# Attention and a gated feed-forward on one core: the values' products ahead of both score steps

## The chip, the cores and the metric

The kernel runs on one core of a Trainium2 chip. The core has five engines that run side by side and meet through semaphores: TensorE (PE in the profile; its weight loads are PEld), VectorE (DVE), ScalarE (ACT), GpSimd (POOL) and SyncE (SP), which issues the transfers here. The metric is the device time of one execution in microseconds (us); less is better.

## The reference

Two stages, in fp32. First attention over 8 batches of 8 heads, with 576 positions and 64 numbers a head. The mask is causal in blocks of 64: a row of block i sees all columns of blocks 0 to i.

```python
scores = scale * np.matmul(q, k.transpose(0, 1, 3, 2))
mask = block_i >= block_j
scores = np.where(mask, scores, -1000000000.0)
scores = scores - np.max(scores, axis=-1, keepdims=True)
attn = np.exp(scores)
attn = attn / (np.sum(attn, axis=-1, keepdims=True) + 1e-09)
return np.matmul(attn, v)
```

The heads of a batch are joined to x (576 x 512), and a gated feed-forward with a residual runs over each batch:

```python
h = gelu(x @ w_in)                     # 512 -> 1024, tanh form
u, v = h[..., :512], h[..., 512:]
v_n = (v - mean(v)) / sqrt(var(v) + 1e-06) * g_ln
v_s = einsum('ts,bsd->btd', w_sg, v_n) + b_sg[None, :, None]
return x + (u * v_s) @ w_out           # 512 -> 512
```

## The kernel before, in words

*Slots.* Attention runs two heads at a time: 32 pairs of heads, one pair a slot, four slots to a batch. Slots 0 to 3 are `opening_slot` (L728), slots 4 to 31 are `slot` (L766). In slot n the kernel finishes the attention of pair n, computes the scores and the softmax of pair n+1, and fills TensorE's time between with pieces of the feed-forward of batches whose attention is done. The tiles of the feed-forward are called accv (first product, v half), accu (u half), accs (the product along the sequence) and acco (the last product).

*A pair's scores.* The 576 rows are cut into five row tiles, 0 to 4 (64 rows, then four times 128); tile i needs 64 + 128 i columns. `Scores.products` (L329) computes them in parts. The contraction is over the 64 numbers of a head, so the two heads lie in the two row halves of the TensorE array: head 0 in rows 0 to 63, head 1 in rows 64 to 127, each writing a bank of its own. Each number is split into a high and a low fp32r part, and three matmuls (high by high, low by high, high by low) add up. `first` (L399) does two parts: 256 columns of tile 4 with tile 1, then the other 320 columns of tile 4 with tile 0. `second` (L403) does tile 3 and then tile 2. A part takes two banks, one for each head, and 6 matmuls for each tile in it: 24 in `first`, 12 in `second`. After the products of a part, `softmax` (L387) issues the maximum on VectorE (`maximum`, L351: adds the mask, writes the scores to SBUF as `prob` and their negated maximum as `negm`) and the exponential on ScalarE (`exponent`, L372, with the sum of each row).

*A pair's values.* In the slot that follows, TensorE turns the probabilities: `va.turn` (L426) makes pA0, pA1, pB0, pB1 and pC, which ScalarE or VectorE copies to SBUF as ptA, ptB and ptC. `turn_sums` (L448) turns the diagonal blocks and the reciprocals of the sums into the banks pd and pe; ScalarE copies both into one tile, rb. `Values.products` (L467) then multiplies the turned probabilities with v: 60 matmuls, head 0 into the left half of the array's columns and head 1 into the right half, row tiles 4 down to 0, into the bank ob; row tile 0 goes to a free part of pe. `normalise` (L484) multiplies ob and that part of pe with the turned reciprocals on VectorE, which gives x, and issues its store (`spill`) on SP's queue. `split` makes the high and low parts of x (xh, xl) later.

*Order of work.* From slot 4 on, TensorE alone is held to the order of the program (`written`, L829, used by `pin`, L83). The order on VectorE, ScalarE and GpSimd is made by a planner which simulates the program with costs of its own; work that comes earlier in the program goes first where both are ready. All PSUM tiles come from one pool of eight banks (L80). `hole(k)` issues the next k pieces of feed-forward; a slot does so after the first transposes, after the second, after `turn_sums` (one piece) and at its end, with counts from `PLAN` and `FIRST` (L718). `load_share` (L709) issues shares of the preparation of weights in slots 4 to 8, at four places of a slot; the third of them, which stands right behind the second score step, has a count of zero in every slot of `WS`.

Of the kernel before, what the change touches and what calls it, by code (L numbers as in the profile page):

```python
# [20 lines left out]
def kernel(  # L21
# [82 lines left out]
    def load_qk(n):  # L104
        b, h = PAIRS[n]
        q_f = sp.tile([P, S], F32, tag="q_f", name="q_f", bufs=1)
        k_f = sp.tile([P, S], F32, tag="k_f", name="k_f", bufs=1)
        nc.sync.dma_start(q_f, qT[b, h : h + 2].rearrange("a d s -> (a d) s"))
        nc.sync.dma_start(k_f, kT[b, h : h + 2].rearrange("a d s -> (a d) s"))
        raw[n] = (q_f, k_f)  # L110

    def split_qk(n):
        out = []
        for x, t in zip(raw.pop(n), "qk"):
            hi = sp.tile([P, S], F32R, tag=t + "h", name=t + "h", bufs=1)
            lo = sp.tile([P, S], F32R, tag=t + "l", name=t + "l", bufs=1)
            if n == 0:
                copy("v" if t == "q" else "a", hi, x)
                vector.tensor_tensor(lo, x, hi.bitcast(F32), op=ALU.subtract)
            else:  # L120
                copy("g", hi, x)
                behind["G"] = gpsimd.tensor_tensor(lo, x, hi.bitcast(F32), op=ALU.subtract)
            out += [hi, lo]
        qk[n] = out

    def load_v(n):
        b, h = PAIRS[n]
        v_f, v_d = vals[n] = v_bufs[n % 2]
        lo, hi = slice(0, BLK), slice(BLK, P)
        for a, r in ((0, lo), (1, hi)):  # L130
            cols = slice((h + a) * D, (h + a + 1) * D)
            x = v[b, : (NT - 1) * P, cols].rearrange("(j p) d -> p j d", p=P)
            if a == 0:
                nc.sync.dma_start(v_f[:, :, r], x)
            else:
                nc.sync.dma_start(v_f[lo, :, r], x[hi])
                nc.sync.dma_start(v_f[hi, :, r], x[lo])
            nc.sync.dma_start(v_d[r, : NT - 1, r], x[lo])
            nc.sync.dma_start(v_d[r, NT - 1, r], v[b, S - TAIL :, cols])
# [162 lines left out]
    def weight_step():  # L302

        while weight_half() is False:
            pass
# [200 lines left out]
    def run_side(k):  # L506

        while k > 0 and side and side[0][0] != "G":
            k -= 1
            side.popleft()[1]()  # L510

    def run_gelu():

        if side and side[0][0] == "G":
            side.popleft()[1]()
# [176 lines left out]
    def hole(k=1):  # L692

        while k > 0 and work:
            try:
                next(work[0])
                k -= 1
            except StopIteration:
                work.popleft()
# [9 lines left out]
    def load_share(n, k):  # L709

        if n in WS:
            with ExitStack() as order:
                for ins in behind.values():
                    order.enter_context(tc.issue_after(ins.ins))
                for _ in range(WS[n][k]):
                    weight_step()
# [5 lines left out]
    def split_pending():  # L722

        for f in pending:
            f()
        pending.clear()
# [39 lines left out]
    def slot(n, va):  # L766
        nx = n + 1 < N
        k = 6 if n // Q == 1 else 3
        g = [int(x) for x in (FIRST if n // Q == 1 else PLAN)[n % Q]]
        if n + 1 < N:  # L770
            load_v(n + 1)
        if n + 2 < N:
            load_qk(n + 2)
        va.turn("A0")
        va.turn("A1")
        hole(g[0])
        run_side(k)
        split_pending()
        load_share(n, 0)
        va.turn("B0")  # L780
        va.turn("B1")
        hole(g[1])
        run_side(k)
        va.turn("C")
        va.turn_sums()
        hole(g[2])
        run_gelu()
        load_share(n, 1)
        if nx:
            nx = Scores(n + 1)  # L790
            nx.first()
        va.products()
        va.normalise()
        if nx:
            nx.second()
        load_share(n, 2)
        if n == Q + 1:
            run_side(2 * NT + 1)
        if n % Q == Q - 1:
            va.split()  # L800
        else:
            pending.append(va.split)
        nv = None
        if nx:
            nv = Values(n + 1, nx)
            nv.inverse()
        if n + 2 < N:
            split_qk(n + 2)
        load_share(n, 3)
        for _ in range(g[3]):  # L810
            hole()
            run_side(k)
        return nx, nv
# [12 lines left out]
    va = Values(0, sc)  # L826
    for n in range(N):
        if n == Q:
            written.intersection_update("P")  # L829
        sc, va = (opening_slot if n < Q else slot)(n, va)  # L830
        if n % (H // 2) == H // 2 - 1:
            v_, u_, s_, o_ = feed_forward(PAIRS[n][0])
            work.extend([v_, u_, *last_o, s_])
            last_o[:] = [o_]
# [47 lines left out]
```

## Time and profile before

| | |
|---|---|
| median of 3 runs | 758.8 us (758.28 to 758.92) |
| the profiled execution | 758.84 us, of which the span from the first to the last instruction is 757.0 us |
| TensorE busy | 735.8 us |
| VectorE busy | 474.8 us |
| ScalarE busy | 425.3 us |
| GpSimd busy | 305.0 us |
| granted TensorE clock, mean | 0.993 |

A row of the profile names the engine, the line, the operation and the tiles as out<-in. Nearly every instruction goes through one helper and so bears the line L60; groups are told apart by their tiles. For a matmul the shape of the array in use stands after the tiles: 128\*128 is the whole array, 64\*128 a row half, 128\*64 a column half. Matmuls are pipelined: the length in a row is longer than the distance to the next start. An idle time stands in brackets behind a row, with what ended it.

### The profile page before, as it was taken

What the parts mean: (1) busy time and instruction counts of PE and PEld (TensorE: products, weight loads), DVE (VectorE), ACT (ScalarE), POOL (GpSimd) and SP (SyncE); (2) the same over time, 40 slices, a digit from 0 to 9 for tenths busy, and PEclk for the clock granted to TensorE, in tenths of its full rate; (3) what the DMA queues carried; (4) which work ended last, traced back from release to release, by engine and by line L of the source; (5) the groups of instructions that cost most, each with busy time, mean ns of one, the idle gap of its engine ahead of it and who ended that gap; (6) DMA issues with size and microseconds to landing.
All of it is one profiled execution on the core that took longest, in us unless ns stands there. A gap on an engine that the chain in (4) does not pass through costs nothing.

```text
span 757.0 us, 18446 instructions
## 1 busy us (share of the span) xinstructions
PE 735.8 (97%) x6946; PEld 693.2 (92%) x6946; DVE 474.8 (63%) x1477; ACT 425.3 (56%) x1064; POOL 305.0 (40%) x376
## 2 busy tenths in 40 slices
PE   8779998999999999999999999999999999999998
PEld 7668998989899899999999899998999989998998
DVE  6988889765855359544785348664495645941732
ACT  5666767457744678337764377544873467721600
POOL 3755697634445323343433334351234532322121
PEclk9979999999999999999999999999999999999999
DMA  6626243333352223322234122521235221120032
GB/s 195 199 69 213 68 121 98 85 95 93 105 160 71 58 79 95 108 69 71 71 118 118 32 71 70 175 75 48 58 85 163 71 57 54 65 78 16 2 126 94
DMA packets 84300, 70.05 MB, mean 93 GB/s; under 512 B 59890, under 2 KB 59890, under 8 KB 84212
## 3 DMA queue, kind: packets, MB, share of 16 engines
q1 hardware_dynamic: 84212, 68.88, 31.0%
q8 instruction: 55, 0.90, 0.5%
q14 instruction: 33, 0.27, 0.1%
HBM read 49.98 MB, written 18.87 MB: 91 GB/s over the span
## 4 chain that ended last, share of the span: by engine, by line
PE 73%; DVE 8%; POOL 5%; DMA 5%; ACT 3%; issue 3%; SPq 2%; DVEq 0%; POOLq 0%; ACTq 0%
PE accs L60 16%; PE acco L60 11%; PE accv L60 11%; PE accu L60 9%; PE s L60 8%; PE ob L60 8%; PE pB L60 3%; PE pA L60 2%; PE pd L60 2%; DVE w L60 2%; ACT prob L60 2%; DVE prob L60 2%; DMA xr<-in_w_out 1%; PE pC L60 1%; POOL rs L60 1%
## 5 line engine op out<-in xcount | busy, mean ns | idle before, releaser
L60 ACT ACTIVATE prob<-prob,negm 128x576 f32<-128x576 f32 (+3 forms) x320 | 176.6, 554 | 70.1 <-DVE negm L60 68.9
L60 DVE CUSTOM_DVE_ANT_0 prob<-s,mask 128x256 f32<-128x256 f32 (+3 forms) x320 | 119.8, 418 | 44.9 <-PE s L60 41.6
L60 POOL TENSOR_TENSOR xh<-x,xh 128x64 fp32r<-128x64 f32 x32 | 10.8, 337 | 196.2 <-DVE xh L60 174.4
L60 POOL TENSOR_TENSOR gl<-u,gh 128x288 fp32r<-128x288 f32 x64 | 52.1, 819 | 88.7 <-DVE gh L60 72.8
L60 PE MATMUL acco<-gh,wo_h 128*128 128x288 f32 x256 | 77.6, 303 | 1.7 <-ACT ptB L60 1.4
L60 PE MATMUL accu<-xh,wi_h 128*128 128x288 f32 x256 | 78.3, 306 | 0.3 <-DVE negm L60 0.3
L60 PE MATMUL accs<-ws_h,vh 128*128 128x288 f32 x256 | 78.0, 305 | 0.0
L60 PE MATMUL accs<-ws_h,vl 128*128 128x288 f32 x256 | 75.5, 295 | 1.7 <-DVE vl L60 1.7
L60 PE MATMUL acco<-gl,wo_h 128*128 128x288 f32 x256 | 75.5, 295 | 0.0
L60 PE MATMUL accu<-xl,wi_h 128*128 128x288 f32 x256 | 75.5, 295 | 0.0
L60 PE MATMUL accs<-ws_l,vh 128*128 128x288 f32 x256 | 75.4, 295 | 0.0
L60 PE MATMUL accu<-xh,wi_l 128*128 128x288 f32 x256 | 75.3, 294 | 0.0
L60 PE MATMUL acco<-gh,wo_l 128*128 128x288 f32 x256 | 75.3, 294 | 0.0
L60 DVE TENSOR_TENSOR u<-accs,u 128x288 f32<-128x288 f32 x64 | 29.2, 457 | 58.3 <-PE accs L60 57.4
L60 PE MATMUL accv<-wi_h,xh 128*128 128x512 f32 x160 | 65.4, 409 | 0.0
L60 PE MATMUL s<-kh,qh 64*128 64x320 f32 (+4 forms) x384 | 64.2, 328 | 0.0
L60 PE MATMUL accv<-wi_l,xh 128*128 128x512 f32 x160 | 62.9, 393 | 0.0
L60 PE MATMUL s<-kh,ql 64*128 64x320 f32 (+4 forms) x384 | 59.8, 305 | 0.9 <-POOL ql L60 0.9
L60 ACT ACTIVATION_READ_ACCUMULATOR prob<-prob,negm 128x1 f32 x320 | 60.0, 188 | 0.0
L60 PE MATMUL s<-kl,qh 64*128 64x320 f32 (+4 forms) x384 | 58.8, 304 | 0.3 <-POOL kl L60 0.3
L60 ACT COPY vv<-accv 128x512 f32<-128x512 f32 x32 | 18.6, 581 | 65.6 <-PE accv L60 65.6
L60 PEld LDWEIGHTS acco<-gh,wo_h 128*128 128x128 f32 x256 | 48.1, 188 | 3.4 <-ACT ptB L60 1.8
(115 smaller groups left out, 2088.5 us busy)
## 6 DMA issues: line engine op xcount, KB each, us to landing
q_f<-in_qT SPq DMA_DIRECT2D x32, 288.0 KB, 3.1
k_f<-in_kT SPq DMA_DIRECT2D x32, 288.0 KB, 3.1
spill<-x SPq DMA_DIRECT2D x32, 288.0 KB, 2.7
xr<-spill SPq DMA_DIRECT2D x32, 288.0 KB, 3.0
out_T<-xr SPq DMA_DIRECT2D x32, 288.0 KB, 2.8
v_f<-in_v SPq DMA_DIRECT2D x32, 128.0 KB, 2.6
v_d<-in_v SPq DMA_DIRECT2D x64, 64.0 KB, 2.7
v_f<-in_v SPq DMA_DIRECT2D x64, 64.0 KB, 2.6
```

Of the source, the lines that this page charges most:

```text
L60: return lambda *a, **k: pin(method(*a, **k), self.letter)
```

## The change

In `slot`, the products of the values and their normalisation move ahead of the first score step, and the two score steps, which stood before and after them, follow one another. Slots 0 to 3 and the work itself stay as they were.

```diff
         hole(g[2])
         run_gelu()
         load_share(n, 1)
+        va.products()
+        va.normalise()
         if nx:
             nx = Scores(n + 1)
             nx.first()
-        va.products()
-        va.normalise()
-        if nx:
             nx.second()
         load_share(n, 2)
         if n == Q + 1:
```

On TensorE a slot with next scores went: feed-forward, 24 score matmuls, 60 products of the values, 12 score matmuls, feed-forward. Now it goes: feed-forward, 60 products, 36 score matmuls, feed-forward. The last slot (31) has no next scores, and nothing changes in it.

## The prediction

> **What bounds the kernel now.** I read the page first (busy time by engine), then the waits of TensorE over the middle of the span, then the instructions of TensorE in order of time around one slot, and last VectorE and ScalarE in the same slot. Times of rows are starts, in us from the start of the span; the second column is the length of the row, and x2 or x16 at its end says how many instructions are merged.
>
> ```profile
> span 757.0 us, 18446 instructions
> PE 735.8 (97%) x6946; PEld 693.2 (92%) x6946; DVE 474.8 (63%) x1477; ACT 425.3 (56%) x1064; POOL 305.0 (40%) x376
> ```
> ```profile
> PE acco L60 <- ACT ptB L60: 1.4, 1, 1.4
> PE acco L60 <- DVE negm L60: 0.4, 2, 0.2
> PE accu L60 <- DVE negm L60: 0.3, 1, 0.3
> ```
>
> The first fence says that TensorE is busy for 97% and the others for two thirds at most. The second is the whole list of what TensorE waited for between 150 and 700 us: 2.1 us in 550. So in the changed stretch the order of TensorE's work and the length of its instructions set the time, and whatever shortens TensorE by a microsecond there shortens the kernel by as much, as long as no new wait comes. Slot 19 shows how a slot looks:
>
> ```profile
> 406.16 0.29 PE L60 MATMUL accs<-ws_l,vone 128*128 128x288 f32 x1
> 406.38 0.38 PE L60 MATMUL s<-kh,qh 64*128 64x256 f32 x2
> 406.61 0.28 PE L60 MATMUL s<-kh,ql 64*128 64x256 f32 x2
> 406.73 0.28 PE L60 MATMUL s<-kl,qh 64*128 64x256 f32 x2
> ...
> 407.64 0.28 PE L60 MATMUL s<-kh,ql 64*128 64x64 f32 x2
> 407.75 0.28 PE L60 MATMUL s<-kl,qh 64*128 64x64 f32 x2
> 407.96 1.09 PE L60 MATMUL ob<-ptA,v_f 128*64 128x128 f32 x16
> 408.88 0.28 PE L60 MATMUL ob<-rb,v_d 128*64 128x64 f32 x4
> ...
> 409.77 0.61 PE L60 MATMUL ob<-ptC,v_f 128*64 128x128 f32 x8
> ...
> 410.54 0.28 PE L60 MATMUL ob<-rb,v_d 128*64 128x64 f32 x4
> 410.66 0.29 PE L60 MATMUL pe<-rb,v_d 128*64 128x64 f32 x4
> 410.87 0.49 PE L60 MATMUL s<-kh,qh 64*128 64x448 f32 x2
> 411.18 0.39 PE L60 MATMUL s<-kh,ql 64*128 64x448 f32 x2
> 411.39 0.39 PE L60 MATMUL s<-kl,qh 64*128 64x448 f32 x2
> ...
> 411.73 0.34 PE L60 MATMUL s<-kh,ql 64*128 64x320 f32 x2
> 411.88 0.33 PE L60 MATMUL s<-kl,qh 64*128 64x320 f32 x2
> 412.14 0.41 PE L60 MATMUL accs<-ws_h,vh 128*128 128x288 f32 x1
> 412.39 0.29 PE L60 MATMUL accs<-ws_h,vl 128*128 128x288 f32 x1
> 412.52 0.29 PE L60 MATMUL accs<-ws_l,vh 128*128 128x288 f32 x1
> ```
>
> The reader is to see three shapes: whole array (128\*128, the feed-forward), row halves (64\*128, the scores, two heads side by side), column halves (128\*64, the values' products). The lengths of rows overlap, so I go by the distance from one start to the next. Each change of shape costs something beyond the ordinary step:
>
> - *Whole to rows.* 406.16 to 406.38 is 0.22, where one such matmul takes 0.13 (412.39 to 412.52): +0.09. The first pair then takes 0.23 (to 406.61) where the next takes 0.12 (to 406.73): +0.11. Together 0.20.
> - *Rows to columns.* 407.75 to 407.96 is 0.21, where the pair before took 0.11 (407.64 to 407.75): +0.10.
> - *Columns to rows.* 410.66 to 410.87 is 0.21, where four such took 0.12 (410.54 to 410.66): +0.09; the first pair takes 0.31 against 0.21 for the next: +0.10. Together 0.19.
> - *Rows to whole.* 411.88 to 412.14 is 0.26 against 0.15 before (411.73 to 411.88): +0.11; the first matmul takes 0.25 against 0.13: +0.12. Together 0.23.
>
> Before: 0.20 + 0.10 + 0.19 + 0.23 = 0.72 us a slot for changes of shape.
>
> **The change, part by part.** *The changes of shape.* In the new order a slot goes whole, columns, rows, whole. Two of the four borders go (whole to rows, rows to columns), and one comes: whole to columns. Slot 31, the last, computes no scores, and so has this border already:
>
> ```profile
> 676.75 0.29 PE L60 MATMUL accs<-ws_l,vone 128*128 128x288 f32 x1
> 676.98 1.09 PE L60 MATMUL ob<-ptA,v_f 128*64 128x128 f32 x16
> ```
>
> The distance is 0.23 against 0.13: +0.10. The sixteen products are as long there as in slot 19 (1.09 in both rows), so the border hides no further cost. After: 0.10 + 0.19 + 0.23 = 0.52. The saving is 0.20 us a slot, uncertain by about 0.02 from rows rounded to 0.01. The two score steps now join inside one visit; the join costs an ordinary pair (0.11 to 0.12, as 407.64 to 407.75). Slots 4 to 30 are changed, 27 of them (32 pairs, the first four go through the other function, the last has no next scores): 27 x 0.20 = 5.4 us, with bounds 4.9 and 5.9.
>
> *The normalisation, its store and the softmax.* VectorE has the same work in another order. In slot 19:
>
> ```profile
> 407.36 0.42 DVE L60 CUSTOM_DVE_ANT_0 prob<-s,mask 128x256 f32<-128x256 f32 x1
> ...
> 408.61 0.55 DVE L60 CUSTOM_DVE_ANT_0 prob<-s,mask,negm 128x320 f32<-128x320 f32 x1
> ...
> 410.94 0.69 DVE L60 TENSOR_TENSOR x<-ob,rb 128x512 f32<-128x512 f32 x1 [1.03 <-PE pe L60]
> 411.55 0.22 DVE L60 TENSOR_TENSOR x<-pe,rb 128x64 f32<-128x64 f32 x1
> ```
>
> Counted from the start of the products (407.96), the normalisation ends at 411.77, that is 3.81 later. It will end 3.81 us after the visit's start instead of 5.39 (411.77 less 406.38), and its store goes to SP's queue earlier by that; the scores issue no DMA, and the shares of weights that stand after them are empty for the place where the store passes, so it passes no other transfer. The maxima, which began 0.98 after the visit's start, will begin at 3.8, so the softmax runs at most 2.84 us later relative to TensorE. No extra time on VectorE or ScalarE: both have idle time in the slot.
>
> *The cover that goes.* The products read copies of the turned probabilities (ptC) and of the turned sums (rb), and until now the first score step, 1.58 us (406.38 to 407.96), stood between. The products need rb 0.92 us after their start (408.88) and ptC 1.81 us after it (409.77). In the ordinary slots both are ready. Two slots of the stretch in which weights are being prepared are late:
>
> ```profile
> 178.87 0.39 PE L60 MATMUL s<-kh,qh 64*128 64x256 f32 x2
> ```
> ```profile
> 179.99 0.57 ACT L60 COPY rb<-pd 128x512 f32<-128x512 f32 x1
> 180.45 0.48 ACT L60 COPY rb<-pe 128x384 f32<-128x384 f32 x1
> ```
> ```profile
> 111.09 0.39 PE L60 MATMUL s<-kh,qh 64*128 64x256 f32 x2
> 112.38 0.38 PE L60 MATMUL s<-kh,ql 64*128 64x256 f32 x2 [0.90 <-POOL ql L60]
> ```
> ```profile
> 113.64 0.68 DVE L60 COPY ptC<-pC 128x512 f32<-128x512 f32 x1
> ```
>
> In slot 9 the products would start at 178.87 and want rb at 179.79; the first copy ends at 180.56 (0.77 late), the second at 180.93 (1.14 late). The first diagonal block lies in the first copy, so I take 0.8. In slot 6 ptC ends at 114.32 and is wanted at 112.90: 1.4 late. But the same slot now loses 1.29 instead of 0.23 on its first pair, waiting for GpSimd's split of q; with the scores 2.9 us later that wait of 1.06 goes. Net 0.4 lost, between 1.4 lost and 1.1 gained if the planner places the copy otherwise.
>
> *The sum.* -5.4 + 0.8 + 0.4 = -4.2. The profiled execution took 758.84 us with a span of 757.0; the 1.8 us around it stay. 758.84 - 4.2 = 754.6, and as the median of the runs is 758.8, the forecast for the median is the same **754.6 us**.
>
> **The rivals.**
>
> *Banks, mild.* The eight banks of PSUM hold, in the new visit, eight tiles of scores beside ob and pe, which are free only once the normalisation has read them. Ten tiles don't fit in eight banks, so the seventh tile of scores waits for the normalisation. It is asked for at 2.91 (410.87 less 407.96, the products and the border) + 1.37 (406.38 to 407.75) + 0.11 + 0.6 (three pairs of 0.21) = 5.0 us after the products' start; the normalisation ends at 3.81. The slack is 1.2 us. Speaking for it is slot 10:
>
> ```profile
> 207.36 0.29 PE L60 MATMUL pe<-rb,v_d 128*64 128x64 f32 x4
> ```
> ```profile
> 209.48 0.68 DVE L60 TENSOR_TENSOR x<-ob,rb 128x512 f32<-128x512 f32 x1
> ```
>
> There VectorE came to the normalisation 1.83 us after the products' last row ended (207.65), behind layer-norm work. If that lateness stays in the seven slots that stand third in their group of four (6, 10 and so on to 30), each loses 1.83 - 1.2 = 0.63, 4.4 in all: 754.6 + 4.4 = **759.0**, no difference. Against it: most of what VectorE did between in slot 10 were this slot's own maxima, which now come after. The Trainium skill speaks against the change at this point: TensorEngine Tiling (Array Packing), section "Gotcha 1: PSUM Pressure", says that row tiling raises the pressure on PSUM, since different row tiles write to different banks. This kernel does have a bank for each head of each part; by that rule alone one visit with eight tiles would be worse than two with four, and what it costs is the 0.63 or 1.4 a slot worked out here, without the page. No wait of the trace in the ordinary slots bears it out yet.
>
> *Banks, hard: slower.* The planner, not the program, orders VectorE in these slots. If it puts the maxima of the first score step ahead of the normalisation, this ends later by about 2.5 us (407.36 to the last maximum, which ends just ahead of 410), so 6.4 instead of 3.8, and TensorE stands for 1.4 us at the seventh tile, with the feed-forward's matmuls queued behind it. It decides from 1.2 us of delay on, and past 1.4 the slot is slower than before. In the seven slots with layer-norm work, where VectorE is full: 7 x 1.4 = 9.8, so 754.6 + 9.8 = **764.4**; in all 27, 792. Against it: the normalisation is ready before any maximum can be, and comes first in the program.
>
> *The softmax too late.* With it 2.84 us later, the next slot's transposes could wait. The shortest distance is in slot 5:
>
> ```profile
> 102.94 1.03 PE L60 MATMUL pA<-ident,prob 128*128 128x128 f32 x8
> ```
> ```profile
> 99.42 0.76 ACT L60 ACTIVATE prob<-prob,negm 128x576 f32<-128x576 f32 x1
> ```
>
> The second head's exponentials end at 100.18, and would at 103.02; its transposes start half-way through the row at 103.4, less 0.2: 103.2. It just holds; a miss costs 0.3 in this slot. In the later groups more of the feed-forward stands between. **754.9**, inside the forecast.
>
> *No stall at all.* If the planner moves rb and ptC forward and the wait for q goes: 758.84 - 5.4 - 1.1 = **752.3**.
>
> *That it doesn't do what it says*: the matmuls are kept in program order, so the borders do go. Only the price of the new one, seen once, could differ; if it cost 0.30 as the two that go do, nothing would be saved but the waits of slots 6 and 9 would stay: 760.0.
>
> **How the numbers follow.** Forecast (with the softmax's 0.3) 0.64; mild bank waits 0.14; hard ones 0.13; no stall 0.07; saving not there 0.02. What a measurement can tell from no change is about 0.2%, 1.5 us: faster is below 757.3, slower above 760.3. Faster: 0.64 + 0.07 = 0.71. No difference: 0.14, with part of the last 0.15. Slower: 0.14. The range: at the low end 752.3 less a rounding, 752.0; at the high end it takes in the mild case, 759.2, and leaves the hard one out. The forecast's own range is 752.9 (saving 5.9, the two slots even) to 756.9 (saving 4.9, slot 6 losing all of 1.4, slot 9 1.1 and 0.5 in softmax and banks).
>
> **What would show it.** Right: in slot 19 the products start 0.23 after the last feed-forward matmul, the scores form one run of 36 matmuls of some 2.6 us, whole matmuls follow 0.26 after it, and from the last whole matmul before to the first one after passes 0.2 less than 5.98 (406.16 to 412.14). Slot 9 shows a wait for rb, slot 6 one for ptC, none for q. VectorE has the normalisation ahead of the slot's maxima. Wrong: waits of TensorE in a score or feed-forward tile for the normalisation or for negm, again and again, or transposes that wait for exponentials; or a border of whole to columns above 0.2.

## The result and the profile after

The median went from 758.54 us (757.59 to 758.92, four runs beside it) to **769.46 us** (768.64 to 771.18, four runs). The ratio is 1.0149, with a 95% interval of 1.0126 to 1.0171: slower by 1.5%, where 754.6 was forecast and 759.2 was the upper end of the range. The profiled execution of the changed kernel took 768.65 us; its page gives the span and the engines:

```profile
span 766.9 us, 18415 instructions
PE 739.4 (96%) x6946; PEld 695.2 (91%) x6946; DVE 472.4 (62%) x1477; ACT 420.9 (55%) x1064; POOL 308.3 (40%) x376
```

TensorE has the same 6946 matmuls. The span grew by 9.9 us, TensorE's busy time by 3.6; the rest is waiting. What TensorE waited for between 150 and 700 us (in us: total, times, longest) is now:

```profile
PE acco L60 <- DVE negm L60: 3.0, 6, 0.5
PE accv L60 <- DVE negm L60: 2.3, 1, 2.3
PE s L60 <- DVE x L60: 1.3, 6, 0.2
```

There were 2.1 us there before, now 6.6. The two rows with a count of six belong together: the first stood at 0.4 before, with a count of two, the last is new. The row with 2.3 is a single wait in slot 8. Slots 4 to 6 lie before 150 us; the waits of slot 6 stand below.

To see where the time went I measured each slot from the first matmul of its visit (the stretch of scores and products between two pieces of feed-forward) to that of the next. In us:

| slots | before | after | difference |
|---|---|---|---|
| 4 | 18.61 | 19.80 | +1.2 |
| 5 | 15.58 | 15.51 | -0.1 |
| 6 | 22.68 | 28.44 | **+5.8** |
| 7 | 24.92 | 24.80 | -0.1 |
| 8 | 20.17 | 23.95 | **+3.8** |
| 9 | 24.22 | 21.81 | -2.4 |
| third of a group from 10 on (10, 14, ... 30) | 22.98 (14) | 24.15 (14) | **+1.2**, the six together +6.5 |
| the other fifteen, 11 to 29 | 24.94, 20.19, 21.94 | 24.80, 20.05, 21.81 | -0.13 or -0.14 (slot 29: -0.37), together -2.2 |
| 31 to the end | 80.05 | 80.06 | 0 |

The sum is +12.4. The profiled span grew by 2.5 less, since the opening (slots 0 to 3, the same program in both) took 74.3 us to the visit of slot 4 instead of 76.9. That stretch came out between 73.9 and 79.9 in the executions below, so a kernel's effect is read better from the slots than from one span; the medians over several runs agree with the slots to within 1.5 us.

**An ordinary slot.** Slot 19 of the changed kernel, TensorE in order of time (start, length, then the matmul):

```profile
414.18 0.29 PE L60 MATMUL accs<-ws_l,vone 128*128 128x288 f32 x1
414.40 1.09 PE L60 MATMUL ob<-ptA,v_f 128*64 128x128 f32 x16
...
417.32 0.39 PE L60 MATMUL s<-kh,qh 64*128 64x256 f32 x2
417.54 0.28 PE L60 MATMUL s<-kh,ql 64*128 64x256 f32 x2
...
418.80 0.45 PE L60 MATMUL s<-kh,qh 64*128 64x448 f32 x2
419.09 0.36 PE L60 MATMUL s<-kh,ql 64*128 64x448 f32 x2
419.29 0.37 PE L60 MATMUL s<-kl,qh 64*128 64x448 f32 x2
...
419.80 0.30 PE L60 MATMUL s<-kl,qh 64*128 64x320 f32 x2
420.03 0.41 PE L60 MATMUL accs<-ws_h,vh 128*128 128x288 f32 x1
```

The order is as forecast, and so is the new border: 414.18 to 414.40 is 0.22, that is 0.09 above a step of 0.13. From the last whole matmul to the next is 5.85 us (414.18 to 420.03) instead of 5.98. So an ordinary slot saves 0.13, not 0.20. The missing part stands at 418.80: the first pair with 448 columns takes 0.29 to the next, which takes 0.20 (419.09 to 419.29), though no shape changes there.

**A third slot.** Slot 14 of the changed kernel, TensorE and then VectorE:

```profile
304.46 0.37 PE L60 MATMUL s<-kl,qh 64*128 64x448 f32 x2
305.03 0.54 PE L60 MATMUL s<-kh,qh 64*128 64x320 f32 x2 [0.21 <-DVE x L60]
...
305.43 0.44 PE L60 MATMUL s<-kl,qh 64*128 64x320 f32 x2
306.37 0.37 PE L60 MATMUL acco<-gh,wo_h 128*128 128x288 f32 x1 [0.50 <-DVE negm L60]
```
```profile
302.78 1.60 DVE L60 SCALAR_TENSOR_TENSOR vl<-vv,rs,vh 128x512 fp32r<-128x512 f32 x2
304.30 0.68 DVE L60 TENSOR_TENSOR x<-ob,rb 128x512 f32<-128x512 f32 x1
...
305.52 0.42 DVE L60 CUSTOM_DVE_ANT_0 prob<-s,mask 128x256 f32<-128x256 f32 x1
```

VectorE comes to the normalisation at 304.30, only behind the layer norm's vl (vv is the value in the layer norm, rs the reciprocal of its deviation, vh and vl the high and low parts of the scaled value). The last tile of scores waits for a bank: 0.57 from the row before (304.46 to 305.03) where such a step takes 0.21 in slot 19. Then the feed-forward waits for the first maximum to give a bank back: 0.94 (305.43 to 306.37) against 0.23 (419.80 to 420.03).

**Slot 6.** TensorE there stops twice:

```profile
114.49 0.66 PE L60 MATMUL ob<-ptC,v_f 128*64 128x128 f32 x8 [2.87 <-DVE ptC L60]
...
115.64 0.39 PE L60 MATMUL s<-kh,qh 64*128 64x256 f32 x2
115.87 0.28 PE L60 MATMUL s<-kh,ql 64*128 64x256 f32 x2
...
124.36 2.21 PE L60 MATMUL pA<-ident,prob 128*128 128x128 f32 x8 [4.16 <-ACT prob L60]
...
127.57 0.44 PE L60 MATMUL accs<-ws_l,vh 128*128 128x288 f32 x1
127.81 0.44 PE L60 MATMUL accs<-ws_h,vh 128*128 128x288 f32 x1
```

The wait for ptC was forecast, at 1.4; it took 2.87. The second, 4.16 for the exponentials, was not forecast for this slot. After it TensorE runs at half clock for some 6 us (the granted clock is 0.50 from 123.52 to 130.34): a step takes 0.24 (127.57 to 127.81) instead of 0.13. Before the change slot 6 had waits too, 3.7 us in three (1.7 for vl, 1.1 for vh, 0.9 for GpSimd's ql), and no half clock; now they are 7.0 in two.

**Slot 8.** VectorE and TensorE in the changed kernel:

```profile
169.08 0.29 DVE L60 TENSOR_SCALAR xr<-xr 128x256 uint32<-128x256 uint32 x1 [2.46 <-DMA xr<-in_w_out]
...
169.99 0.42 DVE L60 CUSTOM_DVE_ANT_0 prob<-s,mask 128x256 f32<-128x256 f32 x1
```
```profile
168.26 0.30 PE L60 MATMUL s<-kl,qh 64*128 64x320 f32 x2
170.84 0.47 PE L60 MATMUL accv<-wi_h,xh 128*128 128x512 f32 x1 [2.27 <-DVE negm L60]
...
171.87 0.63 PE L60 MATMUL accv<-wi_h,xh 128*128 128x512 f32 x1
172.30 0.63 PE L60 MATMUL accv<-wi_h,xl 128*128 128x512 f32 x1
...
175.27 0.39 PE L60 MATMUL accv<-wi_h,xh 128*128 128x512 f32 x1
175.50 0.39 PE L60 MATMUL accv<-wi_l,xh 128*128 128x512 f32 x1
```

VectorE works in order. A piece of weight preparation stands ahead of the maxima and waits 2.46 us for its load; the maxima, whose first scores were done some 2 us earlier, wait behind it, the eight tiles of scores keep their banks, and the feed-forward cannot start. Then for 3.4 us (granted clock 0.50 from 171.30 to 174.72) a step takes 0.43 (171.87 to 172.30) instead of 0.23 (175.27 to 175.50), another 1.6 us.

### The profile page after: what moved, and what is told of

The parts are those of the page before. It is cut to its first block, busy times and chain, and to the rows that moved or that the text cites. A ratio compares the mean times of both kernels' runs of the same rounds, so it can differ in the third digit from the quotient of the medians.

```text
span 766.9 us, 18415 instructions
## 1 busy us (share of the span) xinstructions
PE 739.4 (96%) x6946; PEld 695.2 (91%) x6946; DVE 472.4 (62%) x1477; ACT 420.9 (55%) x1064; POOL 308.3 (40%) x376
## 4 chain that ended last, share of the span: by engine, by line
PE 66%; DVE 13%; ACT 7%; POOL 5%; DMA 4%; issue 3%; SPq 2%; DVEq 0%; ACTq 0%; POOLq 0%
PE accs L60 16%; PE accv L60 13%; PE acco L60 8%; PE ob L60 7%; PE accu L60 7%; PE s L60 5%; ACT prob L60 4%; POOL rs L60 4%; PE pA L60 3%; PE pB L60 3%; PE pd L60 2%; DVE bs L567 2%; DVE vl L60 2%; DVE prob L60 2%; DVE x L60 1%
## 5 line engine op out<-in xcount | busy, mean ns | idle before, releaser
L60 DVE CUSTOM_DVE_ANT_0 prob<-s,mask 128x256 f32<-128x256 f32 (+3 forms) x320 | 117.6, 415 | 5.0 <-PE pd L60 2.5
L60 DVE TENSOR_TENSOR x<-ob,rb 128x512 f32<-128x512 f32 x32 | 22.1, 689 | 82.2 <-PE pe L60 52.5
```

The lines of the kernel that those rows point to most:

```text
L60: return lambda *a, **k: pin(method(*a, **k), self.letter)
```

## The experiments

All of them keep the whole computation and choose, slot by slot, between the old order and the new; 4, 5, 8 and 9 also move one small piece of work. Each gives the ratio to runs of the kernel before on the same chip with its 95% interval, and in the trace the difference to before from slot 4's visit to the end (the changed kernel: +12.4).

**1. The new order from slot 11 on.** This edit against the changed kernel is the frame of all others but the fourth:

```diff
+        together = n >= 11
+        if nx and not together:
+            nx = Scores(n + 1)
+            nx.first()
         va.products()
         va.normalise()
         if nx:
-            nx = Scores(n + 1)
-            nx.first()
+            if together:
+                nx = Scores(n + 1)
+                nx.first()
             nx.second()
```

> The new order in slots 11 to 30 only, the old one in 4 to 10. Theory (VectorE is behind in a few slots, and TensorE waits there): slots 14, 18, 22, 26 and 30 lose about 1.2 us each, the other fifteen save 0.13 each, so 3 to 4 us slower than before: 761.5 to 762.5. Rival (the new order costs a little in every slot, by the row visit itself): 20 of the 27 changed slots carry 20/27 of the loss of 10.9, 766.6.

Ratio 1.0041 (1.0024 to 1.0059), 760.83 against 757.44 us; +3.3 in the trace. That is the 3 to 4 us of the theory: the slots without preparation of weights lose by themselves, since their savings don't pay for the third ones.

**2. The new order up to slot 10.**

```diff
-        together = n >= 11
+        together = n <= 10
```

> The new order in slots 4 to 10 only. Theory: most of the loss lies here, in slots 6 and 8 (waits for ptC, for the exponentials, and for a weight chunk in VectorE's queue): 6 to 7 us slower than before, 764.5 to 765.5. Rival (a loss in every slot): 7/27 of 10.9, 761.4.

Ratio 1.0111 (1.0079 to 1.0143), 766.77 us; +9.6 in the trace. Together with the first it makes 12.9, near the 12.4 of both: most of the loss lies in slots 4 to 10, and weights are prepared in five of them (4 to 8). The loss was larger than the 6 to 7 us expected. Up to slot 10 this kernel issues the same work in the same order as the changed kernel on every engine, and slot 6 took 29.48 here, not 28.44, with 6.4 us of waiting for the exponentials, 1.1 for ptC and 0.8 for ql; in the fourth experiment it took 28.13. So the loss of slot 6, and how it divides into waits, changes by a microsecond or more from one execution to the next.

**3. From slot 11 on, but third slots in the old order.** If the banks of the third slot were the cause, this would keep the savings and lose nothing (Q is 4, so n % Q is 2 in the third slot of a group).

```diff
-        together = n >= 11
+        together = n >= 11 and n % Q != 2
```

> The new order in slots 11 to 30, but not in those that stand third in their group of four (14, 18, 22, 26, 30). Theory: fifteen slots save 0.13 us each and nothing waits: 2 us faster than before, 756.5. Rival (a loss in every slot): 15/27 of 10.9 slower, 764.6.

Ratio 1.0032 (1.0017 to 1.0047), 760.46 us; +2.6 in the trace. The expectation failed: slot 14, now in the old order, still took 23.95 us instead of 22.98. So the loss shows in the third slot and is made before it. It falls on the theory of the banks as the root, and turned the search to the second slot.

**4. All slots new, but in slot 8 the second share of weights moved behind the visit's third place.**

```diff
-        8: (0, 2, 0, 3),
+        8: (0, 0, 2, 3),
```

> The changed kernel, with the two weight steps of slot 8 that stood ahead of the products moved behind the second score step. Theory: VectorE no longer waits for a weight's transfer ahead of the maxima, so the wait of 2.3 us in slot 8 and the half clock after it (about 1.6 us) go: 3 to 4 us faster than the changed kernel, 765.5 to 766.5. Rival (the banks alone make the wait there): no difference from the changed kernel, 769.5.

Ratio 1.0174 (1.0134 to 1.0214), 770.49 us; +13.6 in the trace. The 3 to 4 us expected didn't come. Slot 8 itself was healed (20.05 instead of 23.95), and the time was given back in the next two (23.79 and 27.50 instead of 21.81 and 24.15). TensorE's waits from slot 7 to slot 10 in this kernel:

```profile
PE ob L60 <- ACT rb L60: 2.8, 1, 2.8
PE s L60 <- DVE x L60: 1.5, 1, 1.5
```

The work that had blocked VectorE in slot 8 blocks it a slot later: VectorE waits 2.37 us for a load of w_out, ahead of slot 9's normalisation, and TensorE's 1.5 follow. The wait of 2.8 for rb lies in slot 10. The cause of slot 8 is confirmed by its wait going, but moving one share is no cure.

**5. From slot 11 on, with the reciprocals of the sums behind the end of the second slot.** In the trace of the changed kernel the chain into slot 14 starts in slot 13. VectorE there, and GpSimd after it, first before and then after the change:

```profile
280.04 0.17 DVE L60 TENSOR_SCALAR r<-sums 128x10 f32<-128x10 f32 x1 [1.21 <-ACT prob L60]
...
280.37 0.64 DVE L567 BATCH_NORM_STATS2 bs<-vv 128x6 f32<-128x512 f32 x1
...
285.56 0.65 POOL L60 TENSOR_SCALAR rs<-stats 128x5 f32<-128x5 f32 x1 [0.68 <-DVE stats L60]
```
```profile
288.09 0.17 DVE L60 TENSOR_SCALAR r<-sums 128x10 f32<-128x10 f32 x1 [2.10 <-ACT prob L60]
...
288.43 0.64 DVE L567 BATCH_NORM_STATS2 bs<-vv 128x6 f32<-128x512 f32 x1
...
293.46 2.64 POOL L60 TENSOR_SCALAR rs<-stats 128x5 f32<-128x5 f32 x1 [1.46 <-DVE stats L60]
```

The reciprocals r need the last exponentials, which are later now: VectorE stands 2.10 us instead of 1.21 at r, and the moments of the layer norm (mean and variance, the row BATCH_NORM_STATS2) behind it begin 10.78 after slot 13's visit (288.43 less 277.65) instead of 8.94 (280.37 less 271.43). Then a small operation of GpSimd takes 2.64 instead of 0.65. Together nearly 4 us, and that is how vl comes to stand in slot 14 ahead of the normalisation. The edit, beside `n >= 11`:

```diff
-            nv.inverse()
+            if n % Q != 1:
+                nv.inverse()
...
             hole()
             run_side(k)
+        if nx and n % Q == 1:
+            nv.inverse()
         return nx, nv
```

> The new order in slots 11 to 30, and in the slots that stand second in their group (13, 17, ...) the reciprocals of the sums are issued at the slot's end, behind the layer-norm's moments, not ahead of them. Theory (the later exponentials of the second slot hold the reciprocals, and with them the moments behind them in VectorE's queue, so that the layer-norm's scaling falls into the third slot's visit): the third slots' loss of about 1.1 us goes, and twenty slots save 0.13 each: 2 to 3 us faster than before. Rival (eight tiles of scores in one visit are too much for the banks of the third slots, whatever came ahead): as with the new order from slot 11 on alone, 3 us slower than before.

Ratio 0.9969 (0.9956 to 0.9983), 755.73 against 757.74 us; -2.7 in the trace. Slot 14 took 22.95 us instead of 24.15. The same stretch in this kernel:

```profile
276.01 0.68 DVE L567 BATCH_NORM_STATS2 bs<-vv 128x6 f32<-128x512 f32 x1
...
283.05 0.57 POOL L60 TENSOR_SCALAR rs<-stats 128x5 f32<-128x5 f32 x1
```
```profile
294.72 0.31 PE L60 MATMUL s<-kh,qh 64*128 64x320 f32 x2
```

The moments come first, 8.27 after slot 13's visit (276.01 less 267.74), GpSimd takes 0.57, and the last tile of scores in slot 14 (second fence) starts with no wait behind its row. With the same eight tiles of scores in one visit the bank wait is gone; so the queue on VectorE in the slot before was the cause, and the banks were where it showed.

The -2.7 meets the 2 to 3 us expected partly by luck. The edit moves the reciprocals in slots 5 and 9 too, which keep the old order: slot 9 got 1.8 shorter by that and slot 10 1.0 longer, and slots 4 to 10 together give -1.0. The other -1.7 come from slot 11 on, not the 2.6 of twenty slots at 0.13: slots 14, 18, 22 and 26 save 0.03 each, and slot 30 loses 0.6. No run moves the reciprocals with the old order everywhere, so what that move is worth by itself isn't known.

**6. From slot 11 on, only first and fourth slots.**

```diff
-        together = n >= 11
+        together = n >= 11 and n % Q in (0, 3)
```

> The new order in slots 11 to 30, but only in those that stand first or fourth in their group (11, 12, 15, 16, ...). Theory (the loss starts in the second slots): nothing waits, ten slots save 0.13 each: 1 to 1.5 us faster than before. Rival (any new order ahead of a third slot delays the layer-norm): 1 us or more slower than before.

Ratio 0.9986 (0.9972 to 1.0000), 756.43 us; -1.4 in the trace, 0.14 a slot for ten slots. Where neither the second nor the third slot is touched, only the saving is left.

**7. From slot 11 on, only third slots.**

```diff
-        together = n >= 11
+        together = n >= 11 and n % Q == 2
```

> The new order in slots 14, 18, 22, 26 and 30 only. Theory (the third slots lose by what the second ones did): the layer-norm is as early as before, so no loss, five slots save 0.13: 0.5 us faster than before, to within 0.5. Rival (the banks of the third slot itself): 5 x 1.2, 6 us slower than before.

Ratio 0.9993 (0.9980 to 1.0007), 757.16 us: no difference that can be told. In the trace slot 14 took 22.87 instead of 22.98. The third slots alone, with eight tiles in one visit, lose nothing.

**8. All slots new but 6 and 8, reciprocals moved as in the fifth.**

```diff
-        together = n >= 11
+        together = n not in (6, 8)
```

> The new order in all slots from 4 on but 6 and 8, with the reciprocals behind the moments in the second slots of a group. Theory (slots 6 and 8 lose by their own order: exponentials too late behind layer-norm work in 6, a weight's transfer ahead of the maxima in 8): 25 slots save 0.13, slot 4 loses about 1: 2 us faster than before. Rival (these losses come from the slots ahead of them): 5 us or more slower than before.

Ratio 1.0008 (0.9997 to 1.0018), 757.89 us; +1.4 in the trace. The 2 us expected didn't come. Slot 8 was normal and slot 9 saved its 2.4, but slot 6, in the old order, still took 27.46 us instead of 22.68. TensorE there:

```profile
114.67 0.58 PE L60 MATMUL s<-kh,ql 64*128 64x256 f32 x2 [4.79 <-POOL ql L60]
```

GpSimd's split of q, which cost 0.90 before, is 4.79 late, and slot 6 isn't at fault. What is left is slot 5 (or 4).

**9. The old order in slots 4, 5, 6 and 8, the new in the others, reciprocals moved from slot 9 on.**

```diff
-        together = n not in (6, 8)
+        together = n == 7 or n >= 9
-            if n % Q != 1:
+            if n < 9 or n % Q != 1:
-        if nx and n % Q == 1:
+        if nx and n >= 9 and n % Q == 1:
```

> The new order in slot 7 and in slots 9 to 30, the old one in 4, 5, 6 and 8, with the reciprocals behind the moments in the slots from 9 on that stand second in their group. Theory: what slots 11 to 30 gained with that (2.6 us) stays, and slots 7, 9 and 10 add 0.1, 0.6 and 1.3: 4 to 5 us faster than before, 753 to 754. Rival (slots 9 and 10 were faster only because slot 8 had handed them its loss): 2.6 us faster than before, as with the new order from 11 on.

Ratio **0.9946** (0.9934 to 0.9959), 753.85 against 758.17 us (753.29 to 755.12 against 757.15 to 760.44); -4.6 in the trace, the 4 to 5 us expected. It beats both kernels. Everything TensorE waited for between 150 and 700 us:

```profile
PE ob L60 <- DVE ptC L60: 0.7, 1, 0.7
```

Slots 4, 5, 6 and 8 took as long as before (18.61, 15.58, 22.55, 20.19) and slot 9 saved its 2.4. Of the others, slots 14, 18, 22 and 26 saved 0.03, slot 10 0.27, slot 29 0.37, and the rest 0.11 to 0.14; slot 30 lost 0.61, and the wait of 0.7 above lies in it.

**10 to 12. One slot alone in the new order.** The slots with the large losses, one at a time:

```diff
-        together = n >= 11
+        together = n == 5
```

> The new order in slot 5 alone. Theory (in slot 5 the loads of the spatial weights come later in SP's queue, behind loads of v that wait for the products and behind the store; GpSimd, which waits for them, splits q and k later, and slot 6 waits): from slot 6's first score or product to slot 7's 4 to 5 us more than the 22.7 of before, 4 to 5 us slower. Rival (slot 6 loses by its own order alone): no difference within 0.5 us.

Ratio 1.0037 (1.0024 to 1.0051), 760.66 us; +3.3 in the trace, less than expected. Slot 5 itself took 15.51, slot 6 26.41: +3.7, in a slot that wasn't changed. SP's queue shows the way. Transfers in the order of issue before, and then after the change (all slots new):

```profile
95.86 2.40 SPq L255 DMA_DIRECT2D xr<-in_w_sgT  x2
98.36 1.12 SPq L139 DMA_DIRECT2D v_d<-in_v  x2
...
104.09 0.58 SPq L490 DMA_DIRECT2D spill<-x  x1
```
```profile
95.36 1.26 SPq L139 DMA_DIRECT2D v_d<-in_v  x2
...
98.09 0.55 SPq L490 DMA_DIRECT2D spill<-x  x1
98.74 0.38 SPq L255 DMA_DIRECT2D xr<-in_w_sgT  x1
```

With the products earlier, the planner puts the next loads of v and the store ahead of the loads of weights, and SP stands at the first of these loads until the products have freed its buffer. In the list of SP's waits after the change:

```profile
SPq L139 <- PE ob L60: 7.5, 1, 7.5
```

Before, the first of these loads of weights went out 0.4 after slot 5's visit began (95.86 less 95.5), now 4.6 after it (98.74 less 94.1). GpSimd starts their split later, and the split of q stands behind it in GpSimd's order. With slot 5 alone in the new order SP's queue has the same sequence (loads of v from 95.69, the store at 98.98, the first load of weights at 100.30), and GpSimd waits for them:

```profile
104.96 0.67 POOL L60 CAST ws_h<-xr 128x576 fp32r<-128x576 f32 x1 [4.22 <-DMA xr<-in_w_sgT]
```

In slot 6 TensorE then waits 2.2 us for ql, where it waited 0.9 before. No run keeps these loads in their old place with slot 5 in the new order: that slot 5 makes the loss is tested, the way through SP's queue is read from the trace.

```diff
-        together = n >= 11
+        together = n == 6
```

> The new order in slot 6 alone. Theory (its softmax comes behind the layer-norm's scaling on VectorE, and slot 7's transposes wait for the exponentials): slot 6 takes 3 to 5 us more than the 22.7 of before, 3 to 5 us slower. Rival (all of slot 6's loss is handed down by slot 5): no difference within 0.5 us.

Ratio 1.0077 (1.0064 to 1.0091), 763.92 us; +6.7 in the trace. Slot 6 took 29.47: +6.8, more than expected. Here the split of q is in time; the chain is VectorE's: maxima behind the layer norm's vl, the exponentials behind the maxima, the next transposes behind the exponentials (two waits of 4.4 in all). With slots 5 and 6 both new slot 6 lost 5.8, 6.8 and 5.5 in three executions (the changed kernel, the second and the fourth experiment), not 3.7 + 6.8: one delay covers the other.

```diff
-        together = n >= 11
+        together = n == 8
```

> The new order in slot 8 alone. Theory (a weight's transfer comes late, and VectorE, which is to convert it, stands ahead of the slot's maxima; TensorE then lacks a bank, and its clock falls to half): slot 8 takes 3 to 4 us more than the 20.2 of before, of which slot 9 gives back some 2; 1.5 us slower in all. Rival (the loss is handed down from slots 4 to 7): no difference within 0.5 us.

Ratio 1.0032 (1.0017 to 1.0047), 761.07 us; +3.3 in the trace. Slot 8 took 24.26 (+4.1) and slot 9 gained 0.7, not the 2 expected, so the whole lost twice the 1.5 us expected. VectorE's wait for the load is there again, with slot 8 alone changed:

```profile
162.84 0.29 DVE L60 TENSOR_SCALAR xr<-xr 128x256 uint32<-128x256 uint32 x1 [2.98 <-DMA xr<-in_w_out]
```

So is the feed-forward's wait for a bank (2.6 us, for negm).

## Why the prediction was wrong

*TensorE sets the time, and a change of order there pays at once.* Right for the slots from 11 to 29 that don't stand third in their group: 15 slots saved 2.2 us. But the list of waits on which it rested began at 150 us, and slots 4 to 6, ahead of that, carry the largest loss.

*0.20 us a slot.* The borders go and come as said, but the term was mis-sized: 0.13. The prediction charged the first pair of 448 columns (+0.10) to the border from columns to rows. It costs 0.09 inside the row visit too. After the change the border still slows a first pair, now the one of 256 columns (417.32 to 417.54, 0.22), so both are paid. 27 slots at 0.13 are 3.5 us, not 5.4.

*"It passes no other transfer."* This step failed. I looked for what the program puts between the old and the new place of the store. On SP the order comes from the planner too, and with the products earlier the loads of v and the store passed the loads of weights. Slot 5 alone in the new order costs 3.7 us in slot 6; that it comes by this way is read from the trace.

*"No extra time on VectorE or ScalarE: both have idle time in the slot."* This step failed, and it is the larger one. The idle time of an engine that works in order is not free if the instruction at its head waits. Later maxima and exponentials put such heads in front: r in the second slots (6.5 us over the six third slots from 10 on; the fifth experiment takes it away in 14 to 26), the preparation of weights behind its load in slot 8 (3.8), vl and the maxima in slot 6 (6.8 alone).

*The cover that goes.* In slot 6 ptC is a wait and the wait for q is gone, as forecast; 2.9 instead of 1.4, behind five centring operations of VectorE that took 6.21 us. In the second experiment, with the same order, ptC was 1.1 and a wait of 0.8 for q stayed, so how far this part of the forecast held differs from one execution to the next. Net 0.4 was forecast for the slot, 5.8 came. In slot 9 the 0.8 for rb did not come: the changed kernel has no wait for rb from 150 us on. Only the fourth experiment shows one (2.8), and that in slot 10.

*Banks, mild.* The right place, at twice the size: 5.85 to 7.14 us (299.23, the last whole matmul before the visit of slot 14, to 306.37) is 1.29 gross, against 0.63. The wait it names, the seventh tile of scores for the normalisation, costs 0.36 (0.57 less 0.21); the larger part, 0.71 (0.94 less 0.23), is the feed-forward's wait for the first maximum behind it, which this rival did not have. The lateness that I had taken from slot 10 came out by luck: in slot 14 the normalisation starts 4.84 after the first product (304.30 less 299.46), as it did in slot 10 before (4.81), but behind vl, which the slot before hands on, and no longer behind maxima. The rule of the Trainium skill that was weighed there (TensorEngine Tiling (Array Packing), "Gotcha 1: PSUM Pressure") names what waits, a bank; by the third, fifth and seventh experiments it isn't what costs: eight tiles in one visit lose nothing when VectorE is on time.

*Banks, hard.* Did not happen: in slot 14 the normalisation (304.30) comes ahead of all maxima (305.52).

*The softmax too late.* It happened, with 4.2 us in slot 6, and not in slot 5 where the margin was worked out. There I moved the exponentials by the 2.84 us of an ordinary slot; in slot 6 the larger maxima stand behind the layer norm's vl in VectorE's order, and the exponentials behind them:

```profile
120.15 1.82 DVE L60 SCALAR_TENSOR_TENSOR vl<-vv,rs,vh 128x512 fp32r<-128x512 f32 x2
121.89 0.54 DVE L60 CUSTOM_DVE_ANT_0 prob<-s,mask,negm 128x320 f32<-128x320 f32 x1
```

TensorE had come to the end of its feed-forward by 120.20 and stood there (124.36 less the wait of 4.16).

*Left out altogether.* Slot 8 (no step looked at what stands at VectorE's head there) and slot 4 (+1.2, with a wait of 0.8 for ptA that wasn't there before; not followed further). The -2.4 of slot 9 wasn't foreseen either: the waits of 1.4 for ptB and 0.3 of accu for negm, shown in the prediction's second fence, went with it; the rest I haven't taken apart. In the ninth experiment slot 30 takes 23.82, where it took 23.21 before the change and slot 14 takes 22.95: a wait of 0.73 for ptC lies in it, which VectorE copies between the layer norm's vl operations; why they come so late in that slot stays open.

## What to carry to other kernels

When TensorE's work is moved in a kernel whose other engines work in order, list for each of them (and each DMA queue) which instruction will now stand at the head and what it waits for; busy shares of two thirds say nothing on that. Price slots with extra work (preparation, layer norm) one by one, not at the rate of the ordinary slot. And where a change loses, try it by classes of slots: the same edit, left out of four slots and with one small operation moved in the slot before the loss, turned +1.5% into -0.5%. How much of that the small operation brings without the new order was not tried.

## What was not expected of the hardware

*A small GpSimd operation that takes 0.6 us or 2.6.* In the changed kernel six of the eight 128x5 rs operations took 2.64, the others 0.56 and 0.65. Before the change two did (195.76 and 646.44, in slots 9 and 29) and the others 0.63 to 0.65; in the fifth and the ninth experiment none took more than 0.65. The long ones run beside VectorE's centring of the layer norm, back-to-back operations with two SBUF inputs: all 38 of them, in fourteen traces, overlap five centrings. But the 0.65 us of slot 13 before the change (285.56) and the 2.64 us there now (293.46) both begin 0.16 after the first centring, so the place of the start alone does not decide. In slot 6 VectorE is slow as well beside GpSimd's work: five centring operations took 6.21 us, where the five in slot 13 take 3.36.

```profile
107.62 6.21 DVE L573 SCALAR_TENSOR_TENSOR vv<-vv,stats,g_bc 128x512 f32<-128x512 f32 x5
```

The Trainium skill (SBUF — State Buffer, section "Who interferes with whom") says that a VectorE instruction with two SBUF inputs contends with a GpSimd instruction that reads SBUF, and that contention on the ports they share is an exclusive lock. The rows agree that both get longer; no run here isolates it, and what decides between 0.6 and 2.64 stays open.

*Half clock after short stops.* In slot 8 a stop with a wait of 2.27 us was followed by 3.4 us at half clock; in slot 6 the stop with a wait of 2.87 was not (115.64 to 115.87 is the ordinary 0.23), the one of 4.16 was. The length of the stop alone does not decide; its place does. The granted clock of the changed kernel goes to 0.50 at 123.52 and 171.30 and back to 1.00 at 130.34 and 174.72. The distances from one to the next (6.82, 40.96, 3.42) are 2, 12 and 1 times 3.41 us, so the clock seems to be set at the ends of fixed steps of that length. In the step up to 123.52 TensorE was idle for 3.31 us, in the one up to 171.30 for 2.27; the wait of 2.87 lies across the end of a step at 113.28 (three steps ahead of 123.52), with 1.66 on one side and 1.21 on the other. In the traces of all fourteen kernels, from 60 us on, the clock fell after each of the nine steps at full clock in which TensorE was idle for 1.76 us or more, and after only one with 1.70 or less (1.60, in the tenth experiment). The Trainium skill (TensorE: Matmul & The Clock Gate, "Part 1: The HAM clock gate (the "warmup" mystery)") gives one idle window of about 3.4 us as the condition; slot 8 stays below that, and 2.27 us were enough here.

*The first pair of 448 columns* takes 0.09 more than the next even behind pairs of the same array shape.
